# Packing the 64 leftover tokens of each even sequence into the half-empty last token block of the next sequence

## The chip, the cores and the metric

The kernel runs on one core of a Trainium2 chip. The metric is the time of one execution on the device, in microseconds (us). The median before is 971.42 us of 3 runs (970.99 to 972.41). The profile shows the span of one execution, from its first to its last instruction, which is about 2 us shorter than that execution's time; the profiled execution of the kernel before (966.1 us) was a quicker one than the three timed. PE is TensorE, PEld its weight loads, DVE VectorE, ACT ScalarE, POOL GpSimd and SP SyncE, whose queue issues most transfers. Sequences and blocks are counted from 0.

Runs of one and the same kernel here spread over several us (the kernel before: 965.2 to 972.96 in one series of 11). In the traces nearly all of that lies ahead of the last block of sequence 0, while weights and filters are still being loaded: that block starts anywhere from 204.2 to 211.1 us in the 14 traces. From there to the end, two traces of one kernel differ by up to 0.25 us; from sequence 2 on, the length of each block agrees to 0.02 us. So this document reads effects of tenths of a microsecond from the traces, block by block, and uses the times only for what they can resolve.

## The reference, cut to what matters

```python
def _attn_ref(x, filt_r, filt_i):            # x: (8, 3008, 256)
    X = np.fft.rfft(x, axis=1)
    Y = X * (filt_r + 1j * filt_i)[None, :, :]
    return np.fft.irfft(Y, n=x.shape[1], axis=1)

def _moe_ref(x, w_gate, w_val, w_out, rms_g):  # x: (24064, 256), d_ff = 1536
    rms = np.sqrt(np.mean(x * x, axis=-1, keepdims=True) + 1e-06)
    xn = x / rms * rms_g
    g = xn @ w_gate
    silu = g * (1.0 / (1.0 + np.exp(-g)))
    return silu * (xn @ w_val) @ w_out
```

Eight sequences of 3008 tokens go through an FFT filter, then every token goes through RMS norm and a SwiGLU layer. 3008 is 47 x 64. The kernel handles 128 tokens per matmul of the second layer: two halves of 64 tokens. As 47 is odd, each sequence ends in a group in which only 64 of 128 tokens are real.

## The kernel before: what the change and the argument touch

Each sequence has 6 token blocks (m = 0 to 5) of four groups of 128 tokens. Every block takes 12 steps (jt), called slots here; 8 x 6 x 12 = 576 slots in all. The last block is 448 tokens wide: 3 full groups and half a group.

```python
def ntok(m):
    return 512 if m < 5 else 448

def gv(b, m, jt):                      # gate and value: 4 matmuls of w columns
    w = ntok(m)
    xn = st[b]["xn"][m]
    pg = psG.tile([P, 512], FP32, tag="pg", name="pg")
    pv = psV.tile([P, 512], FP32, tag="pv", name="pv")
    for ps, wt in ((pg, wg), (pv, wv)):
        for dt_ in range(2):
            nc.tensor.matmul(ps[:, 0:w], wt[:, dt_, ts(jt, P)], xn[:, dt_, 0:w], ...)
    # cut: silu on ACT (sg), product with pv on DVE (hh)

def down(b, m, jt):                    # runs two slots behind gv
    # cut: at jt == 0 the two accumulators po0, po1 are taken (one buffer each)
    for s4 in range(4):                # 4 matmuls of 256 columns, also in the last block
        nc.tensor.matmul(po[s4 // 2][:, s4 % 2, :], hh[:, ts(s4, P)], wo[:, jt, :], ...)
    if jt == JT - 1:
        o3 = op.tile([P, 4, D], FP32, tag="o3", name="o3")
        nc.scalar.activation(out=o3[:, 0:2, :], in_=po[0], func=AXT.Copy)
        if m < 5:
            nc.vector.tensor_copy(out=o3[:, 2:4, :], in_=po[1])
        else:
            nc.vector.tensor_copy(out=o3[:, 2, :], in_=po[1][:, 0, :])
            nc.vector.tensor_copy(out=o3[0:64, 3, :], in_=po[1][0:64, 1, :])
```

While one sequence goes through these slots, the FFT of the following ones is woven in at fixed slots. The parts: `psb` (forward transform, PE), products with the filter on DVE (L223 and two of L243), their sum `s` on POOL (L246), `psi` (second transform, PE) `lag` slots after its `psb`, `psn` (inverse transform), `psq` (sum of squares), then `rho` (POOL), two transfers through memory that spread rho over all partitions, and the scaling `xn` on POOL.

```python
elif b == 2:
    a_at = [22 + 2 * i for i in range(12)]
    b_at = [50 + 4 * i for i in range(16)]       # psb
    lag, t4_at, n_at = 4, 118, 123               # psi at b_at + lag; token loads; psn
else:                                            # sequences 3 to 7
    ...
    lag, t4_at, n_at = 8, t + 46, t + 51
```

`psi` and `psn` take turns on one PSUM bank (a buffer that matmuls write to), `psb` and `psq` on another.

## Time and profile before

| what | value | view |
|---|---|---|
| span of the profiled run | 966.1 us | page |
| PE busy | 884.5 us (92%) | page |
| PE busy from 205 to 960 us, granted clock (1.00 is full speed) | 749.57 of 755 us, 1.00 | windows |
| a slot 512 wide; in a last block, 448 wide (no FFT work in it) | 1.30 us; 1.19 us | timeline |
| four down matmuls | 0.44 us | timeline |

The page of the kernel before, cut: engines (busy us, share of the span, instructions), the chain of waits that ended last, and groups of instructions (busy us, mean ns | idle time before them and what ended it).

```profile
PE 884.5 (92%) x6095; PEld 553.0 (57%) x6095; DVE 668.8 (69%) x1047; ACT 632.9 (66%) x1066; POOL 376.8 (39%) x325
...
PE 77%; DMA 8%; issue 5%; POOL 4%; DVE 4%; ACT 2%; SPq 0%; POOLq 0%; DVEq 0%; ACTq 0%
...
L398 PE MATMUL po<-wo,hh 128*128 128x256 f16 x2304 | 348.3, 272 | 1.7
...
L367 POOL TENSOR_TENSOR xn<-y,rb 128x1024 f16<-128x1024 f32 x46 | 132.2, 2873 | 54.9 <-DMA rb<-r_tmp 44.6
```

PE is nearly always busy after 205 us. The mean of 272 ns of a down matmul is its time in flight, not its cost: they overlap, and four start every 0.44 us, so one costs 109 ns.

The view by windows of the kernel before, for the last blocks of sequences 0 and 2: the stretch, its length, then busy us of each engine with its number of instructions, granted clock, share of DMA engines, GB/s.

```profile
core 0: us, PE busy (x) PEld busy (x) DVE busy (x) ACT busy (x) POOL busy (x), PEclk, DMA share, GB/s
204.76:223.35 18.59, 17.79 (x141) 11.71 (x139) 14.44 (x25) 13.59 (x24) 9.39 (x8) 1.00 0.42 102
424.79:441.76 16.97, 16.97 (x133) 11.61 (x131) 14.06 (x24) 13.66 (x25) 8.36 (x7) 1.00 0.45 97
```

In sequence 2 PE never rests. In sequence 0 it already does. The timeline of PE in sequence 0's last block, in the kernel before, shows why: start, length, instruction, and in brackets the idle time before it and what ended it.

```profile
207.54 0.35 PE L304 MATMUL psq<-ones,sq 128*128 128x1 f16 x8
...
208.78 0.38 PE L255 MATMUL psi<-s,wi 128*128 128x256 f16 x2
...
214.93 0.38 PE L255 MATMUL psi<-s,wi 128*128 128x256 f16 x2 [0.34 <-POOL s L246]
...
221.27 0.38 PE L255 MATMUL psi<-s,wi 128*128 128x256 f16 x2 [0.33 <-POOL s L246]
```

And the timeline of POOL for the same stretch of the same kernel:

```profile
208.89 1.03 POOL L310 TENSOR_TENSOR rho<-u,mhalf 128x4 f32<-128x4 f32 x1 [0.17 <-DVE u L308]
213.73 1.15 POOL L246 TENSOR_TENSOR s<-s,s 128x512 f16<-128x512 f16 x1 [3.81 <-DVE s L243]
217.24 2.87 POOL L367 TENSOR_TENSOR xn<-y,rb 128x1024 f16<-128x1024 f32 x1 [2.37 <-DMA rb<-r_tmp]
220.06 1.16 POOL L246 TENSOR_TENSOR s<-s,s 128x512 f16<-128x512 f16 x1
```

The reader should see a chain here: psq at 207.54, rho at 208.89, then the transfers, xn when the rho transfer lands, the next sum right behind xn, and psi at 221.27 as soon as that sum is there. It takes 13.73 us, of which 5.5 us pass between the issue of the second transfer and its landing (the view by tile of rb).

### The profile page before, as it was taken

The numbers are of one execution on the slowest core, as the hardware profiler recorded it, in microseconds if no ns is written. First come the engines' busy times: TensorE is split into PE (matmuls) and PEld (weight loads), VectorE is DVE, ScalarE is ACT, GpSimd is POOL, SyncE is SP. The second block draws the span as 40 slices with busy tenths as digits, with TensorE's granted clock in tenths as the row PEclk, the third lists the DMA queues.
The fourth block names the chain that finished last, engine by engine and source line by source line (L and its number), as shares of the span: only waits on it lengthen the run. The fifth ranks groups of instructions, "written<-read, shape, count | busy, mean of one in ns | idle before, by whom it ended". The sixth has DMA issues, their size and how long they took to land.

```text
span 966.1 us, 17361 instructions
## 1 busy us (share of the span) xinstructions
PE 884.5 (92%) x6095; PEld 553.0 (57%) x6095; DVE 668.8 (69%) x1047; ACT 632.9 (66%) x1066; POOL 376.8 (39%) x325
## 2 busy tenths in 40 slices
PE   3345978999999999999999999999999999999997
PEld 1223545565655666666666666566666666666654
DVE  6632445577777888687877878787878888555554
ACT  6343667677766776677766776677756776566543
POOL 3474325325451445335542545135522554033200
PEclk9576999999999999999999999999999999999999
DMA  8869674664447444754457524743345333422211
GB/s 196 142 123 175 152 166 111 151 169 90 91 109 173 94 94 97 161 136 92 93 119 162 123 84 90 174 94 75 99 110 118 88 61 66 113 50 59 44 44 42
DMA packets 94839, 106.99 MB, mean 111 GB/s; under 512 B 17112, under 2 KB 69464, under 8 KB 94560
## 3 DMA queue, kind: packets, MB, share of 16 engines
q1 hardware_dynamic: 85104, 87.92, 37.7%
q0 software_dynamic: 9552, 17.77, 12.0%
q8 instruction: 48, 0.79, 0.4%
q14 instruction: 39, 0.32, 0.1%
q10 hardware_dynamic: 96, 0.20, 0.1%
HBM read 70.62 MB, written 49.90 MB: 125 GB/s over the span
## 4 chain that ended last, share of the span: by engine, by line
PE 77%; DMA 8%; issue 5%; POOL 4%; DVE 4%; ACT 2%; SPq 0%; POOLq 0%; DVEq 0%; ACTq 0%
PE po L398 23%; PE pg L382 22%; PE pv L382 21%; PE psi L255 3%; PE psb L215 2%; DMA fi<-in_filt_i_dram 2%; PE psn L286 2%; PE psa L194 2%; DMA rb<-r_tmp 2%; DVE hh L387 1%; POOL s L246 1%; DVE o L404 1%; PE psq L304 1%; DMA wv<-in_moe_w_val_dram 1%; DMA xc<-in_x_dram 1%
## 5 line engine op out<-in xcount | busy, mean ns | idle before, releaser
L387 DVE TENSOR_TENSOR hh<-pv,sg 128x512 f16<-128x512 f32 (+1 forms) x576 | 391.6, 680 | 233.7 <-ACT sg L386 111.1
L386 ACT ACTIVATE sg<-pg 128x512 f16<-128x512 f32 (+1 forms) x576 | 338.9, 588 | 241.9 <-PE pg L382 225.1
L398 PE MATMUL po<-wo,hh 128*128 128x256 f16 x2304 | 348.3, 272 | 1.7
L382 PE MATMUL pg<-xn,wg 128*128 128x512 f16 (+1 forms) x1152 | 338.4, 375 | 0.0
L382 PE MATMUL pv<-xn,wv 128*128 128x512 f16 (+1 forms) x1152 | 338.4, 375 | 0.0
L398 PEld LDWEIGHTS <-hh 128*128 128x128 f16 x2304 | 220.9, 98 | 113.0 <-issue 12.9
L246 POOL TENSOR_TENSOR s<-s,s 128x512 f16<-128x512 f16 x96 | 110.7, 1153 | 358.7 <-DVE s L243 296.8
L382 PEld LDWEIGHTS <-wv 128*128 128x128 f16 x1152 | 112.8, 98 | 131.7 <-issue 1.4
L367 POOL TENSOR_TENSOR xn<-y,rb 128x1024 f16<-128x1024 f32 x46 | 132.2, 2873 | 54.9 <-DMA rb<-r_tmp 44.6
L243 DVE TENSOR_TENSOR s<-psb,fi 64x512 f16<-64x512 f32 x192 | 132.1, 688 | 6.0
L382 PEld LDWEIGHTS <-wg 128*128 128x128 f16 x1152 | 109.2, 98 | 12.6 <-issue 0.6
L260 ACT ACTIVATE t<-psi 96x512 f16<-96x512 f32 x128 | 75.5, 593 | 25.7 <-PE psi L255 14.0
L291 ACT ACTIVATE y<-psn,gsb 128x512 f32<-128x512 f32 x94 | 64.7, 688 | 13.2 <-PE psn L286 5.2
L310 POOL TENSOR_TENSOR rho<-u,mhalf 128x4 f32<-128x4 f32 x48 | 49.1, 1023 | 59.8 <-DVE u L308 59.5
L255 PEld LDWEIGHTS <-wi 128*128 128x128 f16 x320 | 32.3, 102 | 62.3 <-issue 26.1
L223 DVE TENSOR_TENSOR s<-psb,fr 128x512 f16<-128x512 f32 x96 | 65.4, 682 | 1.2 <-PE psb L215 0.7
L196 ACT ACTIVATE t<-psa 128x512 f16<-128x512 f32 x96 | 56.4, 599 | 13.1 <-PE psa L194 7.5
L215 PE MATMUL psb<-t,wb 96*128 96x256 f16 x256 | 51.5, 285 | 8.9 <-DMA t<-z_tmp 8.3
L296 ACT ACTIVATE sq<-psn 128x512 f16<-128x512 f32 x94 | 55.6, 591 | 0.0
L255 PE MATMUL psi<-s,wi 128*128 128x256 f16 x256 | 46.2, 272 | 8.0 <-ACT sq L296 3.9
L194 PE MATMUL psa<-xc,wa 128*128 128x512 f16 x96 | 36.7, 397 | 17.2 <-DMA xc<-in_x_dram 8.8
L286 PEld LDWEIGHTS <-t 128*128 128x128 f16 x376 | 29.2, 99 | 22.1 <-issue 1.2
(60 smaller groups left out, 382.5 us busy)
## 6 DMA issues: line engine op xcount, KB each, us to landing
out_dram<-o SPq DMA_DIRECT2D x88, 256.0 KB, 3.3
z_tmp<-t SPq DMA_DIRECT2D x128, 96.0 KB, 2.2
t<-z_tmp SPq DMA_DIRECT2D x32, 384.0 KB, 5.0
g_tmp<-t SPq DMA_DIRECT2D x64, 192.0 KB, 3.2
t<-g_tmp SPq DMA_DIRECT2D x126, 96.0 KB, 2.6
rb<-r_tmp SPq DMA_DIRECT2D x46, 256.0 KB, 4.2
xc<-in_x_dram POOLq DMA_DIRECT2D x56, 192.0 KB, 5.6
out_dram<-o SPq DMA_DIRECT2D x8, 192.0 KB, 3.1
```

Of the source, the lines that this page charges most:

```text
L215: nc.tensor.matmul(ps[:, u, :], wb[:, k, :], st[b]["t2"][k // KC][:, k % KC, :], start=True, stop=True)
L223: nc.vector.tensor_tensor(out=s1, in0=ps, in1=f1, op=ALU.mult)
L243: nc.vector.tensor_tensor(out=s2[a], in0=ps[e], in1=f2[e], op=ALU.mult)
L246: nc.gpsimd.tensor_tensor(out=s, in0=s1, in1=s2, op=ALU.add)
L255: nc.tensor.matmul(ps[:, u, :], wi[:, 2 * i + u, q, :], ss[q][:, u, :], start=(q == 0), stop=(q == n - 1))
L260: nc.scalar.activation(out=st[b]["t3"][c][:, 2 * r:2 * r + 2, :], in_=ps[0:KR], func=AXT.Copy)
L291: nc.scalar.activation(out=y[:, dh, :], in_=ps, func=AXT.Identity, scale=gsb[:, dh:dh + 1])
L367: nc.gpsimd.tensor_tensor(out=xv, in0=yv, in1=rv.unsqueeze(1).to_broadcast([P, 2, 4, P]), op=ALU.mult)
L382: nc.tensor.matmul(ps[:, 0:w], wt[:, dt_, ts(jt, P)], xn[:, dt_, 0:w], start=(dt_ == 0), stop=(dt_ == 1))
L386: nc.scalar.activation(out=sg[:, 0:w], in_=pg[:, 0:w], func=AXT.Silu)
L387: nc.vector.tensor_tensor(out=hh[:, 0:w], in0=pv[:, 0:w], in1=sg[:, 0:w], op=ALU.mult)
L398: nc.tensor.matmul(po[s4 // 2][:, s4 % 2, :], hh[:, ts(s4, P)], wo[:, jt, :], start=(jt == 0 and s4 % 2 == 0), stop=(jt == JT - 1 and s4 % ...
```

## The change

The intent: let even sequences do only the three full groups in their last block (384 columns), and put their 64 leftover tokens into the unused half of the last group of the next, odd sequence, whose last block becomes 512 wide (below this is called the ride). The gate and value columns of a pair stay 896; one of eight groups of down matmuls goes. The diff, cut to its core:

```diff
 def t4_load(b, c):
+    w = XC - 1 if c == NXC - 1 else XC
     ...
-            dma_start(t[p0:p0 + 32, :, :], g_d[b, :, r0:r0 + XC, :])
+            wh = XC if (b % 2 and not h) else w
+            dma_start(t[p0:p0 + 32, 0:wh, :], g_d[b, :, r0:r0 + wh, :])
+            if wh < XC and b % 2:
+                nc.sync.dma_start(t[p0:p0 + 32, wh, :], g_d[b - 1, :, ri * SL + H - 1, :])

-def ntok(m):
-    return 512 if m < 5 else 448
+def nq(b, m):
+    return 3 if (m == 5 and b % 2 == 0) else 4
 # cut: psn, psq, the evictions, rho and xn work on nq(b, m) groups

 def gv(b, m, jt):
-    w = ntok(m)
+    w = nq(b, m) * P

 def down(b, m, jt):
-    for s4 in range(4):
+    n = nq(b, m)
+    for s4 in range(n):
     ...
-        if m < 5:
-            nc.vector.tensor_copy(out=o3[:, 2:4, :], in_=po[1])
-        else:
-            nc.vector.tensor_copy(out=o3[:, 2, :], in_=po[1][:, 0, :])
-            nc.vector.tensor_copy(out=o3[0:64, 3, :], in_=po[1][0:64, 1, :])
+        nc.vector.tensor_copy(out=o3[:, 2:n, :], in_=po[1][:, 0:n - 2, :])

 def o_store(b, m):
     ...
-        w = 3 if (h and m == 5) else 4
+        w = 3 if (m == 5 and (h or b % 2 == 0)) else 4
     ...
+    if m == 5 and b % 2:
+        prev = out[(b - 1) * N:b * N, :].rearrange("(n2 n1) d -> n2 n1 d", n1=N1)
+        nc.sync.dma_start(prev[:, H - 1, :], o3[64:P, 3, :])
```

More of the change, by code (lines that the diff above doesn't have):

```diff
@@ L125 @@
     g_d = nc.dram_tensor("g_tmp", (B, K2, KR, D), FP16, kind="Internal").ap()
-    r_d = nc.dram_tensor("r_tmp", (B, 6, P, 4), FP32, kind="Internal").ap()
+    r_d = nc.dram_tensor("r_tmp", (B, 6, P * 4), FP32, kind="Internal").ap()
     glob = ctx.enter_context(tc.tile_pool(name="glob", bufs=1))
@@ L271, in t4_load @@
                 r0 = ri * SL + h * H + c * XC
-                (nc.scalar if b == 0 and c == 0 and h else nc.sync).dma_start(t[p0:p0 + 32, :, :],
-                                                                   g_d[b, :, r0:r0 + XC, :])
+                wh = XC if (b % 2 and not h) else w
+                (nc.scalar if b == 0 and c == 0 and h else nc.sync).dma_start(
+                    t[p0:p0 + 32, 0:wh, :], g_d[b, :, r0:r0 + wh, :])
+                if wh < XC and b % 2:
+                    nc.sync.dma_start(t[p0:p0 + 32, wh, :], g_d[b - 1, :, ri * SL + H - 1, :])
         st[b]["t4"][c] = t
-    def ntok(m):
-        return 512 if m < 5 else 448
+    def nq(b, m):
+        return 3 if (m == 5 and b % 2 == 0) else 4
     def n_unit(b, m, dh):
@@ L283, in n_unit @@
         ps = bank(0, "psn")
-        for q in range(4):
+        w = nq(b, m) * P
+        for q in range(nq(b, m)):
             n1p = 4 * m + q
@@ L290, in n_unit @@
             st[b]["sq"][m] = sqp.tile([P, 2, 512], FP16, tag="sq", name="sq")
-        nc.scalar.activation(out=y[:, dh, :], in_=ps, func=AXT.Identity,
+        nc.scalar.activation(out=y[:, dh, 0:w], in_=ps[:, 0:w], func=AXT.Identity,
                              scale=gsb[:, dh:dh + 1])
@@ L295, in sq_unit @@
     def sq_unit(b, m, dh):
-        nc.scalar.activation(out=st[b]["sq"][m][:, dh, :], in_=st[b]["sq"].pop((m, dh)),
+        w = nq(b, m) * P
+        nc.scalar.activation(out=st[b]["sq"][m][:, dh, 0:w], in_=st[b]["sq"].pop((m, dh))[:, 0:w],
                              func=AXT.Square)
@@ L301, in q_unit @@
         ps = psB.tile([P, 4], FP32, tag="mb", name="psq")
-        for q in range(4):
+        n = nq(b, m)
+        for q in range(n):
             for dh in range(2):
@@ L307, in q_unit @@
         rho = up.tile([P, 4], FP32, tag="rho", name="rho")
-        nc.vector.tensor_scalar(out=u, in0=ps, scalar1=1.0 / D, scalar2=1e-6 * Y_SCALE * Y_SCALE,
+        nc.vector.tensor_scalar(out=u[:, 0:n], in0=ps[:, 0:n], scalar1=1.0 / D, scalar2=1e-6 * Y_SCALE * Y_SCALE,
                                 op0=ALU.mult, op1=ALU.add)
-        nc.gpsimd.tensor_tensor(out=rho, in0=u, in1=mhalf, op=ALU.pow)
+        nc.gpsimd.tensor_tensor(out=rho[:, 0:n], in0=u[:, 0:n], in1=mhalf[:, 0:n], op=ALU.pow)
         st[b]["u"][m] = rho
     def rho_move(b, m):
-        nc.sync.dma_start(r_d[b, m], st[b]["u"].pop(m))
+        n = nq(b, m)
+        nc.sync.dma_start(r_d[b, m, 0:n * P].rearrange("(p q) -> p q", q=n),
+                          st[b]["u"].pop(m)[:, 0:n])
     def rho_load(b, m):
-        rb = rp.tile([P, P, 4], FP32, tag="rb", name="rb")
-        nc.sync.dma_start(rb.rearrange("p a q -> p (a q)"),
-                          r_d[b, m].rearrange("p q -> (p q)").partition_broadcast(P))
+        rb = rp.tile([P, 4 * P], FP32, tag="rb", name="rb")
+        w = nq(b, m) * P
+        nc.sync.dma_start(rb[:, 0:w], r_d[b, m, 0:w].partition_broadcast(P))
         st[b]["u"][m] = rb
@@ L363, in xn_unit @@
         xn = xnp.tile([P, 2, 512], FP16, tag="xn", name="xn")
-        yv = y.rearrange("p a (q t) -> p a q t", q=4)
-        xv = xn.rearrange("p a (q t) -> p a q t", q=4)
-        rv = rb.rearrange("p t q -> p q t")
-        nc.gpsimd.tensor_tensor(out=xv, in0=yv, in1=rv.unsqueeze(1).to_broadcast([P, 2, 4, P]),
+        n = nq(b, m)
+        yv = y[:, :, 0:n * P].rearrange("p a (q t) -> p a q t", q=n)
+        xv = xn[:, :, 0:n * P].rearrange("p a (q t) -> p a q t", q=n)
+        rv = rb[:, 0:n * P].rearrange("p (t q) -> p q t", q=n)
+        nc.gpsimd.tensor_tensor(out=xv, in0=yv, in1=rv.unsqueeze(1).to_broadcast([P, 2, n, P]),
                                 op=ALU.mult)
@@ L375, in gv @@
     def gv(b, m, jt):
-        w = ntok(m)
+        w = nq(b, m) * P
         xn = st[b]["xn"][m]
@@ L395, in down @@
         po = po_of[(b, m)]
-        for s4 in range(4):
+        n = nq(b, m)
+        for s4 in range(n):
             nc.tensor.matmul(po[s4 // 2][:, s4 % 2, :], hh[:, ts(s4, P)], wo[:, jt, :],
-                             start=(jt == 0 and s4 % 2 == 0), stop=(jt == JT - 1 and s4 % 2 == 1))
+                             start=(jt == 0 and s4 % 2 == 0),
+                             stop=(jt == JT - 1 and (s4 % 2 == 1 or s4 == n - 1)))
         if jt == JT - 1:
```

## The prediction

> **What bounds the kernel now.** TensorE. The page gives PE 884.5 of 966.1 us (92%), DVE 69%, ACT 66%, POOL 39%; from 100 us on, the view by windows gives PE 840.5 of 866 us at a granted clock of 1.00. The chain that ended last is PE for 77%. In the timeline a feed-forward step (one jt) is four gate/value matmuls and four down matmuls: 512 wide it takes 1.30 us, in a last block (448 wide) 1.19 us. Four down matmuls start every 0.44 us, 109 ns each. That agrees with the Trainium skill, "TensorE: Matmul & The Clock Gate", section "Wait — 56ns, not 53.3ns?": columns over 2.4 GHz plus about 2.5 ns, which is 109 ns for 256 columns.
>
> **What changes** (sequences counted from 0).
> - Gate and value: even last block 448 -> 384 columns, odd 448 -> 512. Sum unchanged (0.107 us a step down, then up).
> - Down: the even last block drops one of four matmuls in 12 steps: 48 in all x 109 ns = 5.2 us. This is the gain.
> - Inverse transform (psn): 8 matmuls fewer, about 54 ns each: 0.4 us. Sums of squares (psq): 8 fewer, about 26 ns each: 0.2 us.
> - ACT, DVE, POOL: silu and product cancel over a pair; the even block's evictions and scaling shrink by a quarter; the last output copy becomes one (0.82 us -> 0.41 even, 0.68 odd). Off the critical path.
> - DMA: eight tiny loads and four small stores more, about 0.5 us of SyncE queue each; hidden except the last.
>
> Gross saving on PE: about 5.8 us (0.6%).
>
> **How much is on the critical path.** Nearly all: PE is saturated in the last blocks (windows: sequences 2 and 4, PE 16.97 of 16.97 us). But the even last block falls from 16.97 to about 14.4 us while DVE has 14.05 us of work there now (about 13.7 after) and ACT 13.7 (about 13.1). Expected losses:
> - Sequence 0's last block (18.59 us, PE 17.79): three times PE already waits 0.2 to 0.5 us at psi for POOL's sum (L246), which hangs on DVE two steps back. The chain from the value matmul to the sum is about 3.1 us and hardly shrinks, while PE's two steps shrink by 0.43 us: each stall grows by about 0.3 us, in sum 1.0 us.
> - Sequences 2 and 4: psq waits for the DVE product that holds the shared bank (0.25 us now): about 0.2 us more each.
> - The tail: the very last block is 512 wide (repaid by sequence 6), the last silu and product take 0.12 us longer, a third store is issued at 0.55 us: about +0.4 us.
>
> Net: 5.8 - 1.0 - 0.4 - 0.4 = about 4.0 us, so 967.4 us, range 965.8 to 969.5. Faster by over 2%: 0.01; within 2%: 0.98; slower by over 2%: 0.01.
>
> **What the profile should show.** Down matmuls 2304 -> 2256; psn 376 -> 368; psq 384 -> 376. Even last blocks shorter by about 2.6 us (sequences 2, 4, 6) but only about 1.6 in sequence 0; odd ones longer by about 1.3 us; other blocks unchanged within 0.2 us. PE's wait at psi on POOL L246 up by about 1 us. DVE share in sequence 2's last block 95% or more. A third store ending the trace.
>
> **What would make it wrong.** If DVE or ACT becomes the bound in the short blocks, each loses up to 1 us more and the result is nearer 969.5. If the stalls do not grow and the last small store lands before the larger one, it is 965.8. If the extra reads delayed the last token loads, psn would wait on DMA; those bytes were written a whole sequence earlier, so I do not expect it.

## The result, and the profile after

The changed kernel took 968.12 us (median of 4 runs, 967.02 to 969.77); the kernel before, in all its runs so far, 971.2 us (970.03 to 972.41). A ratio here compares the fast runs of the two kernels in the same rounds, so it is not the ratio of the medians (0.9968). It is 0.9984, with an interval of 0.9959 to 1.0009; a second series (the first experiment) gave 1.0001, 0.9976 to 1.0027. All runs are fast, that is, within 1.5% of the fastest of their kernel. So the median fell in the forecast range, but the times show no gain clear of their noise, and the traces below show about 1 us instead of the 4.0 us that I forecast.

The page of the changed kernel, the lines that answer to those of before:

```profile
PE 880.0 (91%) x6031; PEld 547.8 (57%) x6031; DVE 668.1 (69%) x1039; ACT 630.1 (65%) x1066; POOL 373.1 (39%) x325
...
PE 70%; DMA 10%; issue 6%; DVE 6%; POOL 4%; ACT 3%; SPq 1%; POOLq 0%; DVEq 0%; ACTq 0%
...
L409 PE MATMUL po<-wo,hh 128*128 128x256 f16 x2256 | 343.2, 272 | 2.7 <-DVE o L415 1.3
...
L377 POOL TENSOR_TENSOR xn<-y,rb 128x1024 f16<-128x1024 f32 (+1 forms) x46 | 128.8, 2800 | 59.2 <-DMA rb<-r_tmp 52.1
```

The work went as counted: 48 down matmuls and 64 matmuls in all are gone. But PE's share of the chain fell from 77% to 70%, DMA and DVE took it, and there is a new wait of the down matmuls for DVE's output copy. The windows of the changed kernel for the same two blocks:

```profile
204.90:223.24 18.34, 15.58 (x131) 10.72 (x129) 13.71 (x24) 12.79 (x24) 9.12 (x8) 1.00 0.40 95
426.05:441.37 15.32, 14.89 (x123) 10.62 (x121) 13.32 (x23) 12.76 (x24) 8.09 (x7) 1.00 0.42 104
```

PE's busy time in sequence 0's last block fell by 2.2 us and the block by 0.25 us: the rest became waiting. Less busy time need not be less time.

Block lengths, from the start of a block's first gate weight load to that of the next block's, from the timelines. "By columns" is what PE's work alone would give: for an even last block 12 x 0.107 us for gate and value and 10 x 0.109 us for down, as down runs two slots behind and its last two slots count in the next block. Ends of traces are read by windows, to 0.01 us; the expectations below took them from the span of the page, which is rounded to 0.1 us, and so give tails up to 0.06 us different.

| stretch | before | after | difference | by columns |
|---|---|---|---|---|
| sequence 0, last block | 18.59 | 18.34 | -0.25 | -2.37 |
| sequence 2, last block | 16.97 | 15.32 | -1.65 | -2.37 |
| sequence 4, last block | 16.97 | 15.09 | -1.88 | -2.37 |
| sequence 6, last block | 15.45 | 13.34 | -2.11 | -2.37 |
| last blocks of sequences 1, 3, 5 | 50.65 | 54.37 | +3.72 | +3.85 |
| last block of sequence 0 to the start of the last slot | 753.26 | 751.84 | -1.42 | about -5.9 |
| start of the last slot to the end of the trace (the tail) | 7.99 | 8.61 | +0.62 | |

The odd blocks pay in full what the even ones do not gain in full. The timeline of PE in sequence 0's last block, changed kernel:

```profile
207.62 0.35 PE L311 MATMUL psq<-ones,sq 128*128 128x1 f16 x8 [0.18 <-DVE s L243]
...
208.85 0.38 PE L255 MATMUL psi<-s,wi 128*128 128x256 f16 x2 [0.21 <-POOL s L246]
...
214.62 0.38 PE L255 MATMUL psi<-s,wi 128*128 128x256 f16 x2 [0.82 <-POOL s L246]
...
221.48 0.38 PE L255 MATMUL psi<-s,wi 128*128 128x256 f16 x2 [1.40 <-POOL s L246]
```

From psq to the third psi it is 13.86 us, as against 13.73 us before, although PE has less to do in between. POOL in the same stretch, and the DVE instruction that completes the third sum's inputs:

```profile
208.90 1.03 POOL L317 TENSOR_TENSOR rho<-u,mhalf 128x4 f32<-128x4 f32 x1
213.42 1.15 POOL L246 TENSOR_TENSOR s<-s,s 128x512 f16<-128x512 f16 x1 [3.49 <-DVE s L243]
217.45 2.87 POOL L377 TENSOR_TENSOR xn<-y,rb 128x1024 f16<-128x1024 f32 x1 [2.88 <-DMA rb<-r_tmp]
220.28 1.15 POOL L246 TENSOR_TENSOR s<-s,s 128x512 f16<-128x512 f16 x1
```

```profile
218.34 0.68 DVE L243 TENSOR_TENSOR s<-psb,fi 64x512 f16<-64x512 f32 x1
```

xn starts when the transfer lands, and the sum that psi needs stands behind xn. The Trainium skill ("TensorE: Matmul & The Clock Gate", section "Architectural detail: the array is 16× 32×32, not 1× 128×128") says that ACT and DVE queues are strictly first in, first out and GPSIMD's is so per Q7 core, and section "Step-by-step: what each phase is for" of that page says that matmuls stay in program order. The trace agrees: the sum's inputs were ready at 219.02 us, but POOL took it only at 220.28 us, behind xn, and PE did nothing during its 1.40 us of waiting.

In sequence 2 the loss is another one. PE and then DVE of the changed kernel at the head of the short block:

```profile
429.52 0.38 PE L409 MATMUL po<-wo,hh 128*128 128x256 f16 x2
430.18 0.27 PE L409 MATMUL po<-wo,hh 128*128 128x256 f16 x1 [0.27 <-DVE o L415]
430.29 0.49 PE L392 MATMUL pg<-xn,wg 128*128 128x384 f16 x2
```

```profile
428.97 0.56 DVE L397 TENSOR_TENSOR hh<-pv,sg 128x384 f16<-128x384 f32 x1
429.44 0.68 DVE L415 COPY o<-po 128x512 f32<-128x512 f32 x1
```

The down matmuls of the new block need po1, and DVE copies the old block's po1 out only from 429.44 us on, because its queue is behind. From the first down matmul to the next gate matmul it is 0.77 us instead of 0.33 us: 0.44 us lost. In the kernel before the four down matmuls at this place took 0.47 us, next to nothing lost. psq, three slots later, loses another 0.32 us to the DVE product that holds its bank (start times in the timeline). The two, 0.76 us, account for the 0.72 us that are missing in sequence 2's last block.

### The profile page after: what moved, and what is told of

Its sections match the earlier page's. It is cut to its first block, busy times and chain, and to the rows that moved or that the text cites. A ratio compares the mean times of both kernels' runs of the same rounds, so it can differ in the third digit from the quotient of the medians.

```text
span 965.5 us, 17242 instructions
## 1 busy us (share of the span) xinstructions
PE 880.0 (91%) x6031; PEld 547.8 (57%) x6031; DVE 668.1 (69%) x1039; ACT 630.1 (65%) x1066; POOL 373.1 (39%) x325
## 3 DMA queue, kind: packets, MB, share of 16 engines
q0 software_dynamic: 9552, 17.77, 12.1%
## 4 chain that ended last, share of the span: by engine, by line
PE 70%; DMA 10%; issue 6%; DVE 6%; POOL 4%; ACT 3%; SPq 1%; POOLq 0%; DVEq 0%; ACTq 0%
PE po L409 21%; PE pg L392 21%; PE pv L392 20%; DVE hh L397 3%; PE psi L255 3%; DMA fi<-in_filt_i_dram 2%; DMA rb<-r_tmp 2%; PE psb L215 2%; PE psn L291 2%; PE psa L194 2%; DVE o L415 1%; DMA t<-g_tmp 1%; POOL s L246 1%; DMA z_tmp<-t 1%; DMA g_tmp<-t 1%
## 5 line engine op out<-in xcount | busy, mean ns | idle before, releaser
L409 PE MATMUL po<-wo,hh 128*128 128x256 f16 x2256 | 343.2, 272 | 2.7 <-DVE o L415 1.3
L409 PEld LDWEIGHTS <-hh 128*128 128x128 f16 x2256 | 216.2, 98 | 112.7 <-issue 13.1
L377 POOL TENSOR_TENSOR xn<-y,rb 128x1024 f16<-128x1024 f32 (+1 forms) x46 | 128.8, 2800 | 59.2 <-DMA rb<-r_tmp 52.1
L392 PEld LDWEIGHTS <-wg 128*128 128x128 f16 x1152 | 109.1, 98 | 13.8 <-issue 1.8
L296 ACT ACTIVATE y<-psn,gsb 128x512 f32<-128x512 f32 (+1 forms) x94 | 63.7, 678 | 12.5 <-PE psn L291 4.8
L317 POOL TENSOR_TENSOR rho<-u,mhalf 128x4 f32<-128x4 f32 (+1 forms) x48 | 48.4, 1009 | 56.5 <-DVE u L315 56.1
L302 ACT ACTIVATE sq<-psn 128x512 f16<-128x512 f32 (+1 forms) x94 | 54.8, 582 | 0.0
```

The source lines that it names most:

```text
L296: nc.scalar.activation(out=y[:, dh, 0:w], in_=ps[:, 0:w], func=AXT.Identity, scale=gsb[:, dh:dh + 1])
L377: nc.gpsimd.tensor_tensor(out=xv, in0=yv, in1=rv.unsqueeze(1).to_broadcast([P, 2, n, P]), op=ALU.mult)
```

## The experiments

My theory: PE's saving is real, but in the even last blocks PE runs into chains that do not get shorter (POOL's sum behind the rho transfer in sequence 0; DVE's queue in 2, 4 and 6), and the saving turns into waiting. Rivals: the short block is bound by the throughput of DVE or ACT; the new small transfers delay others; the dropped matmuls had not cost what I charged.

**e1: the changed kernel again.** No edit.

> The changed kernel again, unaltered, for a tighter interval. Both theories expect the same time: the trace shows 1.4 us less than before from the last block of sequence 0 to the end of the last step, and 0.7 us more in the tail, so 0.5 to 3 us less than before, with a spread of 1 to 2 us that comes from the start.

Measured: 969.62 us (6 runs, 965.92 to 970.82), ratio 1.0001. Sequence 0's last block was 18.24 us, and the other even last blocks 15.32, 15.09 and 13.36 us. Up to the start of the last slot it was 751.58 us, the tail 8.62 us. The blocks repeat; the time does not resolve the difference.

**e2: the dropped down matmul put back.**

```diff
-        for s4 in range(n):
+        for s4 in range(4):
```

> Undo only the dropped down matmul: even last blocks do the fourth one again on stale columns (never stored; the result stays right). Theory (PE saved 5.2 us but part of it became waiting in the even last blocks): the added work fills waits that are there anyway. Sequence 0's last block stays within 0.5 us of 18.34 us, those of sequences 2, 4 and 6 grow by 0.8 to 1.1 us, in all about +3 us. Rival (the dropped matmuls were saved in full and the loss is elsewhere, in DMA or the tail): +5.2 us, 1.3 us in each pair, sequence 0 included.

Measured: ratio 1.0037 (1.001 to 1.0064) to before. The even last blocks became 18.48, 16.09, 15.87 and 14.44 us: +0.24, +0.77, +0.78 and +1.08 us against e1. From sequence 0's last block to the start of the last slot it was 754.47 us, 2.9 us more than e1. So 5.2 us of matmul work put back costs about 3 us, and in sequence 0 nearly nothing. The rival (5.2 us, sequence 0 included) falls.

**e3: no ride.** The result is wrong: the store of 256 rows is left out.

```diff
-                wh = XC if (b % 2 and not h) else w
+                wh = XC if b % 2 else w
-        if m == 5 and b % 2:
+        if False:
```

> Undo only the ride: odd sequences load their own padding row again and the store to the previous sequence is left out, so 256 rows of the output are wrong on purpose; all compute instructions stay. Theory: the loads and stores of the ride cost nothing but the last store: blocks unchanged within 0.2 us, the tail after the last matmul 0.5 us shorter. Rival (the extra small transfers delay the token loads or the rho transfers): the even and the following blocks become 2 us or more shorter in sum.

Measured: ratio 0.9985 (0.9962 to 1.0008). Sequence 0's last block 18.23 us; the tail fell from 8.62 to 8.12 us, as expected. Four blocks were 0.22 to 0.25 us shorter than in e1 (in sequences 2, 4, 5 and 6), about 0.9 us in sum, which I had not expected. In all four the timeline puts it at the down matmuls that wait for DVE's output copy: in sequence 4's fourth block 0.51 us in e1 and 0.29 us here, as in the kernel before. But e5 below keeps the ride and has the same shorter blocks (15.09 in sequence 2, 13.12 in sequence 6), so the ride alone does not make this step of 0.22 us. What moves it is open. The rival, which needed 2 us or more, falls but for the tail.

**e4: lag 6 for sequence 2.**

```diff
-    lag, t4_at, n_at = 4, 118, 123
+    lag, t4_at, n_at = 6, 120, 123
```

> In the changed kernel, sequence 2's second transform (psi) is placed 6 slots after its first one instead of 4 (and its token loads 2 slots later). Theory (in sequence 0's last block psi waits 2.4 us for POOL's sum, which waits behind the scaling that waits for the rho transfer): those waits go, sequence 0's last block falls from 18.34 to about 16.2 us, and the first three blocks of sequence 1, which hold the same psi at the same lag, by up to 0.8 us each: in all -3 to -4 us. Rival (the short block is bound by DVE or ACT throughput): within 0.5 us of the changed kernel.

A miss: ratio 1.0021, sequence 0's last block 17.91 us instead of about 16.2, and the first three blocks of sequence 1 longer (20.77, 21.48, 19.61). PE waits for POOL's sum no more in that block, but 2.2 us for ACT's square: lag 6 puts psi one slot behind psn, with which it shares a bank, and ACT has to read that bank twice first. One wait was changed for another. The experiment decides nothing between the theories; it says that this lag is not usable.

**e5: xn of sequence 1's first block on DVE.**

```diff
-    nc.gpsimd.tensor_tensor(out=xv, in0=yv, ...)
+    (nc.vector if (b, m) == (1, 0) else nc.gpsimd).tensor_tensor(out=xv, in0=yv, ...)
-    at(s1 + d, fn, b, m)
+    at(70 if (fn == xn_unit and (b, m) == (1, 0)) else s1 + d, fn, b, m)
```

> In the changed kernel one instruction moves: the scaling (xn) of the first block of sequence 1 goes from POOL to DVE and two slots before its use. Theory (from the psq in slot 61 of sequence 0 to the third psi in slot 70 there is a chain of rho, two transfers, xn and sum on POOL that takes 13.8 us before and after the change, whatever PE has to do, so nothing that PE saves there counts): POOL's sum no longer stands behind xn, the third psi wait falls from 1.3 or 1.4 us to 0.2 to 0.8 us, and sequence 0's last block from 18.3 to about 17.4 us; the first two psi waits (0.2 and 0.8 us) stay. Rival (the short block is bound by the throughput of DVE): DVE gets over 1 us more work, so the block stays or grows.

Measured: ratio 0.9967 (0.9938 to 0.9996). PE in this run, the third psi and the first gate matmul of the next block:

```profile
226.51 0.38 PE L255 MATMUL psi<-s,wi 128*128 128x256 f16 x2 [0.31 <-POOL s L246]
...
228.97 0.59 PE L392 MATMUL pg<-xn,wg 128*128 128x512 f16 x2 [0.32 <-DVE xn L377]
```

The third psi's wait fell from 1.30 us (e1) to 0.31 us, the first two stayed (0.20 and 0.82 us), and from psq to the third psi it is 12.77 us instead of 13.76. So one instruction taken out of POOL's queue takes 1.0 us off this chain. Half of it is lost again at once, as the next block's first gate matmul now waits for xn on DVE, 0.49 us by start times. Counted between first gate matmuls, the block fell from 18.25 to 17.74 us; the count by weight loads, 17.25 us, leaves this wait out, as the load ran ahead of it. DVE got 2.0 us more work and the block became shorter, so DVE's throughput does not bound it.

**e6: lag 8 for sequence 2, in the changed kernel.**

```diff
-    lag, t4_at, n_at = 4, 118, 123
+    lag, t4_at, n_at = 8, 122, 127
-    (2, 4, 6, 10) if b > 1 else (2, 3, 4, 7))
+    (2, 4, 6, 10) if b > 2 else (2, 3, 4, 8) if b == 2 else (2, 3, 4, 7))
```

> Lag 6 was a miss: it put psi one slot behind psn, with which it shares one PSUM bank. Here the changed kernel gets lag 8 for sequence 2, the lag that sequences 3 to 7 have (its token loads and inverse transform 4 slots later). Theory (short lag is what ties PE to POOL's sums): the psi waits in sequence 0's last block go, it falls from 18.3 to 16.0 to 16.5 us, and sequence 1's first three blocks (20.0, 19.4, 19.0) come near those of sequence 3 (18.6, 18.2, 17.8): -2 us and about -3 us. Rival (DVE or ACT throughput bounds these blocks): under 0.5 us in sequence 0's last block.

Measured: 960.53 us, ratio 0.9906 (0.9889 to 0.9923). Sequence 0's last block is 15.60 us, and sequence 1's first three are 18.01, 18.65 and 17.77. The timeline of PE in that block, e6:

```profile
207.81 0.35 PE L311 MATMUL psq<-ones,sq 128*128 128x1 f16 x8 [0.18 <-DVE s L243]
...
213.63 0.38 PE L255 MATMUL psi<-s,wi 128*128 128x256 f16 x2
...
218.93 0.38 PE L255 MATMUL psi<-s,wi 128*128 128x256 f16 x2
```

From psq to the third psi it is 11.12 us instead of 13.8, and no psi waits. The block lost 2.6 us with nearly the same work (DVE 13.38 us after 13.64 in e1, ACT 12.72 in both), so the rival of their throughput falls here.

**e7: the same lag 8 in the kernel before.** The same edit.

> The same lag 8 in the kernel before. Theory: here PE had less waiting to lose, so sequence 0's last block falls by only about 1 us (18.6 to about 17.3), and the gain of the change in that block, 0.3 us at lag 4, is 1.1 to 1.5 us at lag 8 (the full saving of the block by the count of columns is 2.4 us; the waits at the output copy and at psq still eat some). Rival (the saving of that block was never on PE's path): the difference of the two kernels in that block stays about 0.3 us.

Measured: 961.36 us, ratio 0.9917 (0.9897 to 0.9937). Sequence 0's last block is 17.47 us. So the change takes 1.87 us from that block at lag 8, more than expected, and 0.25 to 0.35 us at lag 4. From that block to the end of the trace the change takes 2.98 us at lag 8 (755.74 to 752.76) and 0.80 to 1.05 us at lag 4 (761.25 to 760.45, and 760.20 in e1). In that block only the slack of the second transform differs between the lags; further on lag 8 also moves sequence 2's token loads and inverse transform. This is the clearest proof that the saving was there and was waited away. As times, the two kernels with lag 8 were run in the same rounds: their medians differ by 0.83 us, within the spread.

**e8: the output copy of the fifth block of even sequences on ACT.**

```diff
+            if m == 4 and b % 2 == 0:
+                nc.scalar.activation(out=o3[:, 2:n, :], in_=po[1], func=AXT.Copy)
+            else:
                 nc.vector.tensor_copy(out=o3[:, 2:n, :], in_=po[1][:, 0:n - 2, :])
```

> In the changed kernel the second output copy of the fifth block of even sequences moves from DVE to ACT: 4 copies of 0.68 us. Theory (at the head of the short block the third down matmul waits for DVE, which is one queue behind: 0.44 us of delay in sequences 2 and 6, 0.22 in 4): that wait goes and the even last blocks of sequences 2, 4 and 6 become 0.2 to 0.5 us shorter each, psq waits less as well. Rival (DVE is only the messenger, ACT's silu is late): no change or longer.

Measured: ratio 0.9954 (0.9933 to 0.9974). The last blocks of sequences 2, 4 and 6 are 14.96, 14.96 and 13.06 us: 0.36, 0.13 and 0.30 us shorter than in e1, the second less than expected. The copy's place in DVE's queue was the cause there; psq's wait stays (0.39 us in sequences 2 and 4, by start times). The trace is 1.3 us shorter than e1's from sequence 0's last block to the last slot (750.31 us). The times show more than that; I put the rest down to the start, which varies, but have not shown it.

**e9: the ride's store on ACT's queue.**

```diff
-            nc.sync.dma_start(prev[:, H - 1, :], o3[64:P, 3, :])
+            nc.scalar.dma_start(prev[:, H - 1, :], o3[64:P, 3, :])
```

> In the changed kernel only the ride's store to the previous sequence is issued from ACT's queue instead of SyncE's. Theory (from the start of the last step to the end of the trace it is 7.99 us before, 8.66 after and 8.11 without the ride's store, so the third store in a row on one queue ends the program 0.55 us later): the tail falls to about 8.1 us, the blocks stay within 0.3 us. Rival (the bytes of the store, not its issue, take the time): the tail stays at 8.6 us.

A miss: the tail is 8.58 us, not 8.1. The third store is now issued together with the first, but it takes 3.4 us to land instead of 2.6, and the second 3.2 us instead of 3.0. The Trainium skill ("Trainium Kernel Development and Optimization", section "Key Constraints") says that all issuing queues share the same 16 DMA engines and issuing from several saves only the sequencer's time; the trace agrees: 0.04 us of the 8.62 us were saved. The tail is longer by the third store, as e3 shows, but not by its place in the queue.

This run also shows what a longer wait can do. The third psi waited 1.63 us; the windows of e9 around it:

```profile
221.00:223.00 2.00, 0.78 (x5) 0.59 (x5) 0.38 (x1) 0.28 (x1) 2.00 (x3) 0.84 0.00 0
223.00:225.00 2.00, 2.00 (x10) 1.14 (x9) 0.69 (x1) 0.81 (x2) 1.25 (x3) 0.50 0.71 21
225.00:227.00 2.00, 2.00 (x15) 1.36 (x13) 1.25 (x2) 1.21 (x3) 0.00 (x0) 0.80 0.36 29
```

The granted clock (the last column but two) fell to 0.50 after the wait, and the block took 20.19 us instead of 18.24. In four other traces of this stretch (after, e1, e2, e11), with waits of up to 1.50 us, it stayed at 1.00. The length of one wait does not decide it alone: in e8 a wait of 1.33 us up to 136.93 us was followed by a clock of 0.50 from 138.7 to 142.1 us, and in the kernel before a wait of 2.56 us up to 95.67 us by none. Ten of the 14 traces have one or two such drops of 3.4 us between 90 and 195 us; they may be part of the spread of the start.

**e10: lag 8, the copy on ACT and the store on ACT's queue together.** The three edits above.

> The changed kernel with the three repairs: lag 8 for sequence 2, the copy of the fifth block of even sequences on ACT, the ride's store on ACT's queue. Theory: the gains add: 744.2 us from the last block of sequence 0 to the last step (lag 8 alone) less about 1.2 us for the copy, tail 8.1 instead of 8.66: about 1.7 us below lag 8 alone in the trace and 3.5 to 4.5 us below the kernel before with lag 8, out of the 5.8 us counted. Rival (the repairs shift waits to one another): no better than lag 8 alone.

Measured: 958.46 us (4 runs, 958.15 to 958.86), ratio 0.9895 (0.988 to 0.991): the lowest median, though by the ratios not clear of e6. From sequence 0's last block to the end of the trace it is 752.34 us, 0.4 us less than lag 8 alone (1.7 us was expected) and 3.4 us less than the kernel before with lag 8. The gains do not add, as the first block of sequence 2 became 0.9 us longer (19.10 after 18.22 us in e6). ACT in e10 at that place:

```profile
332.41 1.90 ACTq L431 DMA_DIRECT2D out_dram<-o  x1
334.41 0.60 ACT L396 ACTIVATE sg<-pg 128x512 f16<-128x512 f32 x1 [1.55 <-PE psn L291]
```

Issuing the ride's store took 1.90 us of ACT's queue here (0.47 to 0.50 us the other three times), silu came behind it, then the DVE products, and psq waited 0.69 us by start times (psa 0.20 us). So the third repair, which had saved 0.04 us in e9, probably cost 0.9 us here, as its rival said; e10 without it was not run.

**e11 and e12: the rho load one slot later, changed kernel and kernel before.**

```diff
-    at(s1 + d, fn, b, m)
+    at(s1 + d + ((b, m) == (1, 0) and fn == rho_load), fn, b, m)
```

> In the changed kernel one transfer on the suspected chain, the load of rho for the first block of sequence 1, is issued one slot (about 1.2 us) later; PE's work is the same. Theory (chain psq - rho - two transfers - xn on POOL - sum - psi ends last in that stretch): psq to third psi grows from 13.8 to about 15 us, the wait at the third psi from 1.3 to 1.4 to about 2.5 us, sequence 0's last block from 18.3 to 19.5 us at full clock. In the run before this one a 1.63 us wait at the same psi was followed by 3 us at half clock; if a wait of this length is enough for that, the block is 21 us or more and the granted clock after the psi is 0.5. Rival (that chain has slack): no change.

> The same one slot delay in the kernel before, where the wait at the third psi is 0.49 us by the start times. Theory: the chain ends last there too, so psq to third psi grows from 13.7 to about 15 us and the block from 18.6 to about 19.8 us, and before and after the change are again equal in that block to within 0.4 us. Rival: slack of PE's work hides it and the block stays.

Both missed their aim: the blocks were 18.45 and 18.66 us, psq to the third psi 13.97 and 13.79 us, much as without the edit (ratios 1.0003 and 0.9989, two runs each). A load is only a place in the SyncE queue, not a time; one slot later in the program did not hold it back (it was issued 1.64 us after the store of rho in e11 and in the changed kernel alike). So the rivals were not tested this way. The runs still repeat the main reading: nine traces at lag 4 with POOL's xn in place (before, after, e1, e2, e3, e8, e9, e11, e12) have 13.67 to 14.10 us from psq to the third psi, whichever of the two kernels it is and whether or not the fourth down matmul is there. The third psi's wait in e11 was 1.50 us, without a drop of the clock.

## Why the prediction was right or wrong

- **Right: the bound and the gross saving.** PE binds, and the counts came as predicted (2304 to 2256 and so on). The 109 ns per down matmul, an estimate by the Trainium skill's sum ("TensorE: Matmul & The Clock Gate", section "Wait — 56ns, not 53.3ns?"), is what the traces show where PE does not wait (four in 0.44 us).
- **Right: the odd blocks.** They grew by 1.25, 1.25 and 1.22 us (forecast: about 1.3).
- **Luck: the time in the range.** 968.12 us lies in 965.8 to 969.5, but the spread of the start is as wide as the gain: the traces show 0.8 to 1.05 us, not 4.0.
- **Wrong, and the step that failed: "each stall grows by about 0.3 us, in sum 1.0 us"** for sequence 0's last block. The mechanism, psi waiting for POOL's sum, was right; its size was not. By start times all the waits of that block grew from 1.44 to 3.56 us, 2.1 us of the 2.37 us that the block should have gained. I had followed the sum back only to DVE "two steps back". For the third psi it hangs on xn and the rho transfer, a chain of 13.7 us that starts at psq; that wait alone grew by 1.1 us, the other two by 0.1 and 0.5 us. e5, e6 and e7 show it. psq's waits in this block, about 0.5 us more, I had counted only for sequences 2 and 4.
- **Wrong by omission: the output copy.** For sequences 2 and 4 I expected 0.2 us each at psq. They lost 0.72 and 0.49 us, and sequence 6, for which I expected nothing, 0.26 us. The new wait is that of the down matmuls for DVE's copy of the block before (0.44 us in sequence 2); e8 shows it. I had called the copy "off the critical path" because it became cheaper. But DVE's queue did not become shorter as PE's slots did. The psq wait of "0.25 us now" in these blocks is not in the trace of before (PE 16.97 of 16.97 us); after the change it is 0.32 us in each. And DVE was not near its limit: 13.32 of 15.32 us in sequence 2's last block (87%), where I had forecast 95% or more.
- **Undersized: the tail.** +0.62 us instead of +0.4: 0.50 us for the third store (e3) and 0.12 us for the wider last silu and product. I had taken only part of the store's issue as visible. Issuing it elsewhere hardly helps (e9).
- **Right, as far as shown: the extra loads.** e3 shows no delay by them but for the open steps of 0.22 us.

In sum: of about 5.9 us by columns, 4.2 to 4.5 us (e1 and the first trace) were lost before the last slot and 0.6 us in the tail; 0.8 to 1.05 us is left in the traces (one of the kernel before, two of the changed one), too small for the times. Of the loss, 3.6 us lies in the even last blocks and is explained above. Of the rest, 0.44 us is two of the 0.22 us steps of e3 (sequences 4 and 5; again waits for the output copy), whose origin is open, and some lies in sequence 1's first two blocks, which vary from run to run.

## What to carry to other kernels

When work is taken off a saturated engine in one stretch, that stretch becomes shorter for every latency chain in it, and software-pipeline distances counted in steps become shorter in time. So for each wait that is already there, follow its releaser back to something that is not the saturated engine, a transfer or another engine's queue, and see whether that chain is as long as the stretch; if it is, lengthen the distance first, and look at what the new place collides with (lag 6 put psi right behind psn). Here the distance alone (lag 8) was worth 0.8 to 0.9%, more than the change, and with it the change kept about three times as much of its gain.

## What the Trainium skill lacked or had wrong

- "TensorE: Matmul & The Clock Gate", section "HAM oscillation — how this bites in real kernels", gives as the rule that PE gaps of over about 3.4 us are to be avoided. Taken alone, it is too lax here: in e9 a wait of 1.63 us was followed by a granted clock of 0.50 and then 0.80 in windows of 2 us, with the block 1.9 us longer, and in e8 one of 1.33 us by 3.4 us at 0.50; waits of 1.40 us (after), 1.50 us (e11) and 2.56 us (before, up to 95.67 us) were not. What else decides it was not tested, nor whether it happens in runs without a profile.
- "DMA: Bandwidth & Descriptors", section "Anatomy of one DMA — SWDGE (gpsimd) path", gives a cost per transfer, for the gpsimd path; the stores here are issued by SyncE and ACT. I found no page that tells what a further small store behind two others costs at the end of a program: a 64 KB store cost 0.50 us of tail (e3), and 0.46 us of it stayed when it was issued from another queue (e9).
- I found no page that warns that a gain on the bound engine can vanish in waits of fixed length next to it: 64 matmuls worth about 5.9 us gave 0.8 to 1.05 us here, and 2.98 us once the waits of one block had slack.
